# Fourier mixing and a gated SwiGLU on one Trainium2 core: gate rows on ScalarE, two splits four steps later, halves in the first item, raw weights one item sooner

## The chip, the core and the metric

The kernel runs on one core of a Trainium2 chip. Its engines run their own queues in order and meet at semaphores: TensorE (PE in the profile; PEld are its weight loads), VectorE (DVE), ScalarE (ACT), GpSimd (POOL) and SyncE (SP). In this kernel SP issues nearly all loads, POOL nearly all stores. The metric is the time of one execution on the device in microseconds (us); several runs are given by their median.

## The reference

`x` has 2048 rows of 512. The result mixes two branches by a gate of each row:

```python
g = sigmoid((x * gate_w).sum(-1, keepdims=True))
a = x @ dft_hid_re.T ; b = x @ dft_hid_im.T
y = dft_seq_re @ a - dft_seq_im @ b           # branch A, real part of a 2-D Fourier transform
out_B = (silu(x @ w1) * (x @ w3)) @ w2        # branch B, inner width 1376
result = g * y + (1 - g) * out_B
```

All is float32.

## The kernel before, in words

**Precision.** Each float32 operand is split in two: a high part (ScalarE copies it into the tensor engine's rounded format, `high`, line 107) and a low part (VectorE subtracts the high part from the source, `low`, line 110). `mm3` (line 124) then makes each product of three matmuls: high by high, high by low, low by high, in this order. `split` is `high` and then `low`; the profile shows all of them under lines 108 and 111 and all matmuls under line 122.

**Seven products in place of eight.** Each product of 2 x 2 blocks is done by a Strassen-like scheme with seven block products and some sums of blocks, made by VectorE ahead of the splits (`T1` to `T4`, `sums_wb`, `sums1`, `sum2`, `sum_c`).

**First half: gate/up.** The list `ITEMS` holds 22 items, a chunk of 128 columns of `w1` and `w3` by a half of the rows of x. Item 0 is written out by hand (lines 409 to 515, eight products). The others run in `gate_up(n)`, seven products of six matmuls. The order of instructions is the program's (`manual_schedule`): the dictionaries `early`, `ahead`, `second`, `mid` and `at_end` hang extra work into marked places of item n. Product numbers in `prod(ps, n, wi, xi, ...)`: weight forms 0 to 2 come from tile `wa`, 3 to 6 from tile `wb`; x forms are `OPS`, so 3 is `T1`, 4 `T2`, 5 `T3`, 6 `T4`. Products 0 and 1 of an item are done `LOOK` = 3 items ahead (`first1`, `first2`).

The forms of `wb` for the next set (`nw`) are made in the item before: `sums_wb` (four sums of 256 columns, VectorE, lines 253 to 256), `high_wb` (ScalarE, 1024 columns) and `low_wb` (VectorE, 1024 columns). Item 1 makes set 2 in this way, and the forms of `wa` for item 5. For sets below `K` = 9 the `wb` is stored to DRAM, and in the second half of the items (`back`) it is loaded again by `load_wb`; only the raw weights for `wa` (three quarters of a tile, 384 KB) come by `load_w`, four items ahead, at the start of `gate_up`, behind `load_wb` on SP's queue. The x operands of the first half are split during item 0 and 1: the low of `T1` in `early`, the split of `T4` in `ahead` of item 1.

**Second half: the transform.** It goes in blocks: four of the sequence transform (kind F), two of the down projection with `w2` (H) and two of the hidden transform (Y). A block has seven products in the order `CHAIN` (`P1`, `P5`, `P6`, `P3`, `P7`, `P2`, `P4`), each in a few steps; a step of block 0 is twelve matmuls. `step(m)` issues the matmuls of step m and then `advance(m)`: loads for step m + 8, the sum for step m + 4 (`sum_c`, lines 682 and 685) and the split of the operand `zo` for step m + 3 (`split_c`). Four buffers hold `zo`. `at(blk, n, f)` hangs extra work ahead of step n of a block.

The stationary operand of the F blocks is x itself, in eight blocks p of two x halves: `A1[p]` (four first forms, made during gate/up) and `A2[p]` (three second forms, made in block 0). For these, block 0 loads the x blocks again (`load_a2`, steps 4 to 11), makes one sum each (`sum2`, steps 7 to 14) and splits three forms (`make_a2` with `forms2`, steps 8 to 15): two forms of 256 columns in one split of 512, and one form of 256. Form 2 is first read by `P7` (steps 16 to 19), forms 0 and 1 by `P2` (from step 20) and `P4` (from 24). Buffers of the x blocks 4 and 5 are `u3` and `c21`.

**Gates.** The scores of the row gates are one more column of `w1`. `load_score` brings them to all partitions (SP for the first half of the rows, at the end of gate/up; POOL for the second, in block 1). `gates(g)` (line 760) makes them gates: a sigmoid (ScalarE, line 763), two rows of 512 each of a gate times -1 plus 1, or times 1 minus 1, written in the pairwise order of the output columns (VectorE, line 766), a sign change (ScalarE, line 769) and two stores (POOL). SP loads them again in `load_gate` ahead of `P6` of a block (line 854).

Of the kernel before, what the change touches and what calls it, by code (L numbers as in the profile page):

```python
# [9 lines left out]
AF = mybir.ActivationFunctionType  # L10
ALU = mybir.AluOpType
# [10 lines left out]
NG = NST // 2  # L22
NC = (F + P - 1) // P
NP2 = (NC + 1) // 2
WARM = 11
LOOK = 3
# [6 lines left out]
def fnet_swiglu_gate_kernel(  # L33
# [20 lines left out]
    nc = tc.nc  # L54
# [25 lines left out]
    def bank(k, name):  # L80
        return psum.tile([P, 512], F32, tag=f"ps{k}", name=name)
# [20 lines left out]
    def free(*tiles):  # L102
        for t in tiles:
            _, places, at = HELD.pop(id(t))
            places.append(at)

    def high(hi, src):
        nc.scalar.activation(hi, src, AF.Copy)  # L108

    def low(hi, lo, src):  # L110
        nc.vector.tensor_sub(lo, src, hi.bitcast(F32))  # L111

    def split(hi, lo, src):
        high(hi, src)
        low(hi, lo, src)
# [25 lines left out]
    def flat(ap):  # L141
        return ap.rearrange("p a n -> p (a n)")
# [30 lines left out]

        nc.vector.tensor_sub(r[:, :256], r[:, 256:512], r[:, :256])  # L174

    def forms2(r, t2):

        r = r.rearrange("p (a n) -> p a n", a=4)
        split(flat(t2[:, 0, 0:2]), flat(t2[:, 1, 0:2]), flat(r[:, 2:4]))
        split(t2[:, 0, 2], t2[:, 1, 2], r[:, 0])  # L180

# [6 lines left out]
    SETS, WSET = [], []  # L190
# [8 lines left out]
    def flat_x(ap):  # L199
        return ap.rearrange("p q n -> p (q n)")  # L200
# [15 lines left out]
    def xo_parts(g, k):  # L216
        o = XO[g][:, :, OPS.index(k)]
        return flat_x(o[:, 0]), flat_x(o[:, 1]), ST[g, k]

    def split_xo(g, k):  # L220
        split(*xo_parts(g, k))

    WS, WA, WB = {}, {}, {}

    def back(w):
        return w >= NC and SETS[w] > 0

    def load_w(w, lo=0, hi=4):
        if lo == 0:
            WS[w] = f4_a.tile([P, 4, 256], F32, tag=f"f4_{4 + w % (LOOK + 1)}", name=f"ws{w}")  # L230
        nc.sync.dma_start(WS[w][:, lo:hi].rearrange("p a n -> p (a n)"),
                          w13[SETS[w], :, lo * 256 : hi * 256])

    def load_wb(w, spare=False):

        WB[w] = (parts(f"wb{w}") if spare else
                 wbp.tile([P, 2, 4, 256], F32R, tag="wb", name=f"wb{w}"))
        nc.sync.dma_start(WB[w].bitcast(F32), wbsp[SETS[w]])
# [4 lines left out]
    def new_wa(w):  # L243

        WA[w] = wap.tile([P, 2, 3, 256], F32R, tag="wa", name=f"wa{w}")

    WU = {}

    def sums_wb(w):

        r = WS.pop(w)
        u = WU[w] = wup.tile([P, 4, 256], F32, tag="wu", name=f"wu{w}")
        nc.vector.tensor_add(u[:, 0], r[:, 3], r[:, 2])
        nc.vector.tensor_sub(u[:, 1], u[:, 0], r[:, 0])
        nc.vector.tensor_sub(u[:, 2], r[:, 0], r[:, 3])
        nc.vector.tensor_sub(u[:, 3], r[:, 1], u[:, 1])

    def wb_parts(w):
        return flat(WB[w][:, 0]), flat(WB[w][:, 1]), flat(WU[w])

    def high_wb(w):
        WB[w] = wbp.tile([P, 2, 4, 256], F32R, tag="wb", name=f"wb{w}")
        high(wb_parts(w)[0], wb_parts(w)[2])

    def low_wb(w):
        low(*wb_parts(w))
        if w < K:
            nc.gpsimd.dma_start(wbsp[w], WB[w].bitcast(F32))

    def prod(ps, n, wi, xi, start, chain=False):  # L270
        w = WSET[n]
        w, wi = (WA[w], wi) if wi < 3 else (WB[w], wi - 3)
        x = XO[ITEMS[n][1]]
        for q in range(2):
            sl = slice(q * P, (q + 1) * P)
            mm3(ps, w[:, 0, wi, sl], w[:, 1, wi, sl], x[:, 0, xi, q, :], x[:, 1, xi, q, :],
                start and q == 0, q == 1, chain)
# [3 lines left out]
    def first1(n):  # L281
        copy_x(n, prod1(n))
# [46 lines left out]
    def store_h(n, k, h):  # L329

        c, g = ITEMS[n]
        j = min(c % (NP2 - 1) if c < NC - 1 else NP2 - 1, NP2 - 1)
        b = 2 * (NP2 - 1 <= c < NC - 1)
        nc.gpsimd.dma_start(hsp[g, b + k, j // 2, :, j % 2 * 512 : (j % 2 + 1) * 512], h)  # L334
# [4 lines left out]
    early, ahead, second, mid, at_end = {}, {}, {}, {}, {}  # L339

    def run(work, n):
        for f in work.get(n, ()):
            f()

    def gate_up(n):
        last = NI - 1
        x, s1 = G.pop(n)
        z = bank(6 + n % 2, f"Z{n}")
        if n == last - 1:

            u2, g1 = (s1p.tile([P, 512], F32, tag="s1", name=f"{k}_{n}") for k in ("u2", "g1"))
        else:
            h = hp.tile([P, 1024], F32, tag="h", name=f"h{n}")
            u2, g1 = h[:, :512], h[:, 512:]
        u4 = u4p.tile([P, 512], F32, tag="u4", name=f"u4_{n}")
        nw = WSET[n + 1] if n < last else 0
        if nw in WB or nw == 0:
            nw = None
        elif back(nw):
            load_wb(nw)  # L360
            nw = None
        wa = WSET[n + LOOK + 1] if n + LOOK < last else 0
        if wa in WA or wa == 0:
            wa = None
        else:
            load_w(wa, 0, 3 if back(wa) else 4)

        prod(x, n, 4, 4, False, True)
        nc.scalar.activation(u2, x, AF.Copy)
        run(early, n)  # L370
        prod(z, n, 5, 5, True, True)
        run(ahead, n)
        nc.scalar.activation(u4, z, AF.Copy)
        run(second, n)
        if nw is not None:
            sums_wb(nw)
        if n + LOOK <= last:
            first1(n + LOOK)
        if nw is not None:
            high_wb(nw)  # L380
        prod(x, n, 3, 3, False, True)
        nc.vector.tensor_add(u4, u4, x)
        if nw is not None:
            low_wb(nw)
        run(mid, n)
        prod(z, n, 2, 6, False, True)
        nc.vector.tensor_add(u2, u2, z)
        nc.vector.tensor_mul(u2, s1, u2)  # L388
        store_h(n, 0, u2)
        if wa is not None:  # L390
            new_wa(wa)
            parts_a = wa_parts(wa, 0, 3)
            high(parts_a[0], parts_a[2])
        if n + LOOK <= last:
            first2(n + LOOK)
        if wa is not None:
            low(*parts_a)
        prod(x, n, 6, 2, False, True)
        nc.scalar.activation(g1, x, AF.Silu)
        put_score(n, 1, x)  # L400
        if n + LOOK <= last:
            gate1(n + LOOK)
        nc.vector.tensor_mul(g1, g1, u4)
        store_h(n, 1, g1)
        run(at_end, n)
# [36 lines left out]
    def xo_half(k, q):  # L442
        i = OPS.index(k)
        return XO[0][:, 0, i, q], XO[0][:, 1, i, q], ST[0, k][:, q * 512 : (q + 1) * 512]
# [72 lines left out]
    def do(work, n, f, *a):  # L517
        work.setdefault(n, []).append(lambda: f(*a))


    do(early, 1, lambda: low(*xo_parts(0, "T1")))
    do(ahead, 1, lambda: split_xo(0, "T4"))
    do(second, 1, free, *(ST[0, b] for b in ("B11", "B21", "B12", "B22")))
    do(second, 1, sum_g, 2, y2)
    do(mid, 1, gate1, 2)
# [48 lines left out]
    A1, A2, XR = [], [], {}  # L574
# [17 lines left out]
    for n in range(NI):  # L592
        if n in W2_AT:
            p = W2_AT.index(n)
# [4 lines left out]
        if n in A1_AT:  # L599
            p = A1_AT.index(n)  # L600
# [9 lines left out]
    n = NI - 1 - LOOK  # L610
# [117 lines left out]
    def load_a2(p):  # L728
# [8 lines left out]
            XR[p] = wide(f"xs{p}")  # L737
        nc.sync.dma_start(XR[p], xn[p])

    def make_a2(p):  # L740
        A2.append(a2.tile([P, 2, 3, 256], F32R, tag=f"a2_{p}", name=f"a2_{p}"))
        r = XR.pop(p)
        forms2(r, A2[p])
        if p >= NG - 2:
            free(r)

    GATES = {}

# [10 lines left out]

    def gates(g):  # L760

        t, ng = GATES.pop(g)
        nc.scalar.activation(t, t, AF.Sigmoid)
        for j, (v, w) in enumerate(((-1.0, 1.0), (1.0, -1.0))):
            b = slice(j * 512, (j + 1) * 512)
            nc.vector.tensor_scalar(ng[:, b].rearrange("p (n a) -> p a n", a=2),
                                    t[:, b].rearrange("p (a n) -> p a n", a=2),
                                    v, w, op0=ALU.mult, op1=ALU.add)
        nc.scalar.activation(t[:, 512:], t[:, 512:], AF.Copy, scale=-1.0)
        nc.gpsimd.dma_start(gsp[g], t)  # L770
        nc.gpsimd.dma_start(ngsp[g], ng)
# [197 lines left out]
    def at(blk, n, f, *a):  # L969
        todo.setdefault(START[blk] + n, []).append((f, a))  # L970
# [5 lines left out]
        at(0, 7 + p, lambda p=p: sum2(XR[p]))  # L976
    for p in range(NG):
        at(0, 8 + p, make_a2, p)

    at(0, 0, lambda: nc.scalar.activation(act0, act0, AF.Sigmoid))  # L980
    at(0, 4, gates, 0)
    at(1, 3, gates, 1)
    late = [(w2, w2sp, p) for p in range(len(W2_AT), NP2)] + [(dd, dsp, p) for p in range(KD)]
    for i, (src, sp, p) in enumerate(late):
        blk, b = 1 + i // 3, i % 3
        n = (10, 17, 24)[b]
# [11 lines left out]
    for p in range(KD):  # L998
        early = p < NG - NP2
# [76 lines left out]
```

## Time and profile before

| | |
|---|---|
| median of three runs | 678.73 us (678.22 to 678.82) |
| the profiled execution's own time | 678.22 us |
| its span, first to last instruction | 676.5 us |
| TensorE busy | 671.2 us (99%), 3101 matmuls |
| TensorE weight loads busy | 582.8 us (86%) |
| VectorE busy | 602.5 us (89%) |
| ScalarE busy | 365.8 us (54%) |
| GpSimd busy | 64.5 us (10%) |
| DMA | 172.54 MB, 255 GB/s in the mean |
| granted TensorE clock | 1.000 |

How to read the lines below. A row of a timeline has the start in us, the time taken, engine and source line, the operation, the tile written and the tiles read, shapes and a count x; in brackets stands the idle time of the engine ahead of it and what ended it. Rows with x over 1 are merged neighbours. A busy matmul shows about 0.38 us because matmuls are pipelined; what counts is how far apart they start. A view of waits gives engine, line, tile, what was waited for, and then us in total, times and longest. The chain goes back from the last instruction by what released each one.

### The profile page before, as it was taken

Reading aid. Unit: us, or ns where it says so; the run is one execution under the profiler, and the core shown is the slowest. Engines: PE = TensorE matmul, PEld = TensorE weight load, DVE = VectorE, ACT = ScalarE, POOL = GpSimd, SP = SyncE. Lnnn points to the kernel's source line nnn. Section 1 sums busy time; section 2 is a strip of 40 time slices with the busy share of each in tenths; the row PEclk is TensorE's granted clock in tenths of the full one; section 3 lists DMA queues with packets and bytes.
Section 4 is the critical chain, followed back from the end, with each engine's and each line's share of the span. In section 5 each row is a group of like instructions: output and inputs, shape, how many; then the busy total and the mean of one; then the engine's idle time right before and its main releaser. Section 6 shows DMA issues by size and latency. Waiting matters only on the chain.

```text
span 676.5 us, 8652 instructions
## 1 busy us (share of the span) xinstructions
PE 671.2 (99%) x3101; PEld 582.8 (86%) x3101; DVE 602.5 (89%) x739; ACT 365.8 (54%) x479; POOL 64.5 (10%) x119
## 2 busy tenths in 40 slices
PE   9999999999999999999999999999999999999998
PEld 6888888888888888888888888888888888888887
DVE  6999988787679999988999899979796897898996
ACT  6675666655446764465554653554445445445551
POOL 0011111121110000001120101100000010000000
PEclk9999999999999999999999999999999999999999
DMA  7575557499998656814697178919986772874942
GB/s 295 207 305 219 218 194 276 184 328 381 420 415 314 240 181 229 315 69 179 241 352 285 74 253 336 374 56 353 391 328 249 291 244 100 311 271 159 338 134 93
DMA packets 45563, 172.54 MB, mean 255 GB/s; under 512 B 5328, under 2 KB 5712, under 8 KB 41680
## 3 DMA queue, kind: packets, MB, share of 16 engines
q1 hardware_dynamic: 32480, 118.11, 47.9%
q0 software_dynamic: 12752, 53.49, 20.1%
q8 instruction: 24, 0.39, 0.2%
q10 hardware_dynamic: 288, 0.39, 0.2%
q14 instruction: 19, 0.16, 0.1%
HBM read 114.82 MB, written 57.16 MB: 254 GB/s over the span
## 4 chain that ended last, share of the span: by engine, by line
PE 87%; DVE 8%; DMA 1%; issue 1%; ACT 1%; SPq 0%; DVEq 0%; ACTq 0%
PE P L122 61%; PE X L122 15%; PE Z L122 8%; PE Y L122 3%; DVE zo L111 3%; DVE a L111 1%; DMA xs_B<-xt 1%; DVE B L682 1%; DVE B L685 1%; DVE wa L111 1%; DVE xs_B L214 1%; DVE xs L174 0%; DVE xo L111 0%; ACT zo L108 0%; DMA out<-zc 0%
## 5 line engine op out<-in xcount | busy, mean ns | idle before, releaser
L122 PE MATMUL P<-zo,a 128*128 128x512 f32 x1344 | 290.9, 379 | 1.0 <-DVE zo L111 1.0
L122 PEld LDWEIGHTS P<-zo,a 128*128 128x128 f32 x1344 | 253.5, 189 | 38.3 <-DVE zo L111 2.4
L108 ACT ACTIVATE zo<-B 128x1024 fp32r<-128x1024 f32 (+1 forms) x182 | 188.2, 1041 | 180.6 <-PE P L122 79.3
L111 DVE TENSOR_TENSOR zo<-B,zo 128x1024 fp32r<-128x1024 f32 (+1 forms) x182 | 217.0, 1200 | 29.4 <-ACT zo L108 28.8
L122 PE MATMUL P<-zo,H 128*128 128x512 f32 x468 | 101.2, 379 | 0.0
L122 PEld LDWEIGHTS P<-zo,H 128*128 128x128 f32 x468 | 88.5, 189 | 12.6
L682 DVE TENSOR_TENSOR B<-B,B 128x1024 f32<-128x1024 f32 (+1 forms) x78 | 92.7, 1188 | 0.1
L122 PE MATMUL X<-xo,wb 128*128 128x512 f32 x378 | 89.0, 380 | 0.2 <-DVE xo L111 0.2
L122 PEld LDWEIGHTS X<-xo,wb 128*128 128x128 f32 x378 | 71.2, 189 | 11.1 <-DVE xo L111 0.6
L122 PE MATMUL P<-zo,Y 128*128 128x512 f32 (+1 forms) x336 | 71.6, 375 | 0.0
L122 PEld LDWEIGHTS P<-zo,Y 128*128 128x128 f32 x336 | 62.7, 189 | 8.7
L334 POOL DMA_DIRECT2D hsp<-h x42 | 23.0, 548 | 120.4 <-DVE h L388 68.0
L685 DVE TENSOR_TENSOR B<-B,B 128x1024 f32<-128x1024 f32 x26 | 31.6, 1217 | 0.0
L122 PE MATMUL X<-xo,wa 128*128 128x512 f32 x126 | 30.9, 380 | 0.0
L122 PE MATMUL Y<-xo,wa 128*128 128x512 f32 x126 | 30.6, 379 | 0.0
L122 PE MATMUL Z<-xo,wa 128*128 128x512 f32 x126 | 30.6, 379 | 0.0
L122 PE MATMUL Z<-xo,wb 128*128 128x512 f32 x126 | 30.6, 379 | 0.0
L122 PEld LDWEIGHTS X<-xo,wa 128*128 128x128 f32 x126 | 23.7, 189 | 3.8 <-DVE wa L111 0.5
L122 PEld LDWEIGHTS Y<-xo,wa 128*128 128x128 f32 x126 | 23.8, 189 | 3.4
L122 PEld LDWEIGHTS Z<-xo,wb 128*128 128x128 f32 x126 | 23.8, 189 | 3.4
L122 PEld LDWEIGHTS Z<-xo,wa 128*128 128x128 f32 x126 | 23.8, 189 | 3.4
L111 DVE TENSOR_TENSOR wa<-ws,wa 128x768 fp32r<-128x768 f32 (+1 forms) x22 | 19.3, 880 | 8.1 <-ACT wa L108 8.0
(145 smaller groups left out, 543.8 us busy)
## 6 DMA issues: line engine op xcount, KB each, us to landing
B<-cc SPq DMA_DIRECT2D x64, 512.0 KB, 6.0
hsp<-h POOLq DMA_DIRECT2D x42, 256.0 KB, 3.6
B<-hsp SPq DMA_DIRECT2D x20, 512.0 KB, 5.6
wbsp<-wb POOLq DMA_DIRECT2D x8, 1024.0 KB, 4.2
wb<-wbsp SPq DMA_DIRECT2D x8, 1024.0 KB, 7.7
B<-zsp SPq DMA_DIRECT2D x16, 512.0 KB, 8.4
H<-w2sp SPq DMA_DIRECT2D x6, 1024.0 KB, 9.5
ws<-w SPq DMA_DIRECT2D x11, 512.0 KB, 4.6
```

What stands on the lines that cost most here:

```text
L108: nc.scalar.activation(hi, src, AF.Copy)
L111: nc.vector.tensor_sub(lo, src, hi.bitcast(F32))
L122: nc.tensor.matmul(ps.rearrange("p (n a) -> p n a", a=2), u, turns(v)[:, some], **kw)
L214: nc.vector.tensor_sub(t, *(ST[g, v] for v in SUMS[k]))
L334: nc.gpsimd.dma_start(hsp[g, b + k, j // 2, :, j % 2 * 512 : (j % 2 + 1) * 512], h)
L682: nc.vector.tensor_add(t, t, RAW[blk, b, q][:, :n])
L685: nc.vector.tensor_sub(t, RAW[blk, "B12", q], t)
```

## The change

- `forms2` takes a set `some`, and can make the split of 512 columns (0) and that of 256 (1) apart. For x blocks 4 and 5 (`IN_TWO`) `make_a2` makes only the second, at its old place (steps 12 and 13), and `rest_a2` the first, ahead of steps 16 and 17.
- `gates` is taken apart. The sigmoid goes from step 4 of block 0 to step 2; the two rows are made by ScalarE (`gate_row`), one ahead of step 3 and one ahead of step 4; the sign change and the stores (`store_gates`) come ahead of step 5. In block 1, where all was ahead of step 3: sigmoid 3, rows 4 and 5, rest 6.
- `wb_parts` gives two halves of 512 columns, so `high_wb` and `low_wb` issue two instructions each, for every set they make.
- In item 1 the u sum (line 382) comes ahead of `sums_wb` and `high_wb`, and the low parts of `T1` and `T4` are made in halves.
- For the last four sets (16 to 19) `load_w` is issued in the item before the one that issued it, behind the other loads at the start of `gate_up`.

```diff
-    def forms2(r, t2):
+    def forms2(r, t2, some):
         r = r.rearrange("p (a n) -> p a n", a=4)
-        split(flat(t2[:, 0, 0:2]), flat(t2[:, 1, 0:2]), flat(r[:, 2:4]))
-        split(t2[:, 0, 2], t2[:, 1, 2], r[:, 0])
+        if 0 in some:
+            split(flat(t2[:, 0, 0:2]), flat(t2[:, 1, 0:2]), flat(r[:, 2:4]))
+        if 1 in some:
+            split(t2[:, 0, 2], t2[:, 1, 2], r[:, 0])
...
     def wb_parts(w):
-        return flat(WB[w][:, 0]), flat(WB[w][:, 1]), flat(WU[w])
+        return [(flat(WB[w][:, 0, i:j]), flat(WB[w][:, 1, i:j]), flat(WU[w][:, i:j]))
+                for i, j in ((0, 2), (2, 4))]
     def high_wb(w):
...
-        high(wb_parts(w)[0], wb_parts(w)[2])
+        for v in wb_parts(w):
+            high(*v[::2])
     def low_wb(w):
-        low(*wb_parts(w))
+        for v in wb_parts(w):
+            low(*v)
...
-        else:
+        elif wa not in WS:
             load_w(wa, 0, 3 if back(wa) else 4)
+        w = WSET[min(n + LOOK + 2, last)]
+        if w - LOOK - 1 >= NC + 1 and w not in WS and w not in WA:
+            load_w(w, 0, 3)
...
-        if nw is not None:
+        if nw is not None and n > 1:
             sums_wb(nw)
         if n + LOOK <= last:
             first1(n + LOOK)
-        if nw is not None:
+        if nw is not None and n > 1:
             high_wb(nw)
         prod(x, n, 3, 3, False, True)
         nc.vector.tensor_add(u4, u4, x)
+        if nw is not None and n == 1:
+            sums_wb(nw)
+            high_wb(nw)
         if nw is not None:
             low_wb(nw)
...
+    def low_halves(k):
+        for q in range(2):
+            low(*xo_half(k, q))
-    do(early, 1, lambda: low(*xo_parts(0, "T1")))
-    do(ahead, 1, lambda: split_xo(0, "T4"))
+    do(early, 1, low_halves, "T1")
+    do(ahead, 1, lambda: high(*xo_parts(0, "T4")[::2]))
+    do(ahead, 1, low_halves, "T4")
...
+    IN_TWO = (NG - 4, NG - 3)
     def make_a2(p):
...
-        r = XR.pop(p)
-        forms2(r, A2[p])
+        forms2(XR[p], A2[p], (1,) if p in IN_TWO else (0, 1))
         if p >= NG - 2:
-            free(r)
+            free(XR.pop(p))
+    def rest_a2(p):
+        forms2(XR.pop(p), A2[p], (0,))
...
     def gates(g):
+        nc.scalar.activation(GATES[g][0], GATES[g][0], AF.Sigmoid)
+    def gate_row(g, j):
+        t, ng = GATES[g]
+        v = 2.0 * j - 1.0
+        b = slice(j * 512, (j + 1) * 512)
+        nc.scalar.activation(ng[:, b].rearrange("p (n a) -> p a n", a=2),
+                             t[:, b].rearrange("p (a n) -> p a n", a=2),
+                             AF.Copy, scale=v, bias=-v)
+    def store_gates(g):
         t, ng = GATES.pop(g)
-        nc.scalar.activation(t, t, AF.Sigmoid)
-        for j, (v, w) in enumerate(((-1.0, 1.0), (1.0, -1.0))):
-            b = slice(j * 512, (j + 1) * 512)
-            nc.vector.tensor_scalar(ng[:, b].rearrange("p (n a) -> p a n", a=2),
-                                    t[:, b].rearrange("p (a n) -> p a n", a=2),
-                                    v, w, op0=ALU.mult, op1=ALU.add)
         nc.scalar.activation(t[:, 512:], t[:, 512:], AF.Copy, scale=-1.0)
...
+    for n, p in enumerate(IN_TWO):
+        at(0, 16 + n, rest_a2, p)
...
-    at(0, 4, gates, 0)
-    at(1, 3, gates, 1)
+    for g in range(2):
+        at(g, 2 + g, gates, g)
+        for j in range(2):
+            at(g, 3 + g + j, gate_row, g, j)
+        at(g, 5 + g, store_gates, g)
```

## The prediction

> **What bounds the kernel now.** I read the page first, then who made TensorE wait, then the chain of waits in order of time, and last the timelines of the two places that this pointed to.
>
> ```profile
> span 676.5 us, 8652 instructions
> ```
> ```profile
> PE P L122 <- DVE zo L111: 1.0, 2, 0.7
> PE wps L414 <- PEq L1065: 0.8, 1, 0.8
> PE X L122 <- DVE xo L111: 0.2, 1, 0.2
> ```
> ```profile
> 254.80 1.15 DVE zo L111
> 255.95 0.04 issue
> 255.99 414.57 PE P L122 x1919
> ```
>
> The profiled execution took 678.22 us: its span of 676.5 and 1.7 around it. The first view has every wait of TensorE that VectorE ended, three in all. The second, the chain, shows that from 255.99 us on nothing but matmuls sets the end: 414.57 / 1919 = 0.216 us for each, one 512-column matmul after another. So whatever the change does behind 256 us is worth nothing unless it makes a new wait, and what it can gain lies ahead of that. Two places lose time there.
>
> The first is the second item of gate/up (TensorE's timeline):
>
> ```profile
> 28.04 0.38 PE L122 MATMUL X<-xo,wb 128*128 128x512 f32 x1
> 28.59 1.35 PE L122 MATMUL X<-xo,wb 128*128 128x512 f32 x5 [0.18 <-DVE xo L111]
> 29.78 1.46 PE L122 MATMUL Z<-xo,wa 128*128 128x512 f32 x6
> 31.07 1.46 PE L122 MATMUL Y<-xo,wa 128*128 128x512 f32 x6
> 32.47 2.88 PE L122 MATMUL X<-xo,wb 128*128 128x512 f32 x12
> 35.19 1.46 PE L122 MATMUL Z<-xo,wb 128*128 128x512 f32 x6
> 36.48 1.66 PE L122 MATMUL X<-xo,wa 128*128 128x512 f32 x6
> ```
>
> Starts should be 0.216 apart, and a group of six busy 5 x 0.216 + 0.38 = 1.46. The one at 28.04 is followed after 0.55: 0.34 lost. The five behind it take 1.35 for 1.24: 0.11. From 31.07 six matmuls should end the turn at 32.37, not 32.47: 0.10. The twelve take 2.88 for 2.76: 0.12. The six at 36.48 take 1.66 for 1.46: 0.20. Together 0.87 us. That is the head's share.
>
> The second is the first transform block:
>
> ```profile
> 207.62 44.47 PE L122 MATMUL P<-zo,a 128*128 128x512 f32 x205
> 252.78 2.86 PE L122 MATMUL P<-zo,a 128*128 128x512 f32 x12 [0.69 <-DVE zo L111]
> 255.99 6.31 PE L122 MATMUL P<-zo,a 128*128 128x512 f32 x28 [0.35 <-DVE zo L111]
> ```
>
> 205 x 0.216 = 44.28, so the next should start at 251.90; it starts at 252.78: 0.88 lost. Twelve more are due at 255.37 and come at 255.99: 0.62. The 28 take 6.31 for 6.21: 0.10. Together 1.60 us. No more than 0.87 + 1.60 = 2.47 us can be gained at these places.
>
> **Transform: gate rows and moved forms.** One step is 12 matmuls, 2.59 us, so 207.62 is step 0, and steps 17 and 18 are the late ones: each waits for VectorE's low part of its operand, and VectorE runs without a break up to there.
>
> ```profile
> 221.55 0.84 DVE L766 TENSOR_SCALAR u2g<-p5g 128x512 f32<-128x512 f32 x2
> 222.26 1.21 DVE L682 TENSOR_TENSOR B<-B,B 128x1024 f32<-128x1024 f32 x1
> 224.09 1.23 DVE L111 TENSOR_TENSOR zo<-B,zo 128x1024 fp32r<-128x1024 f32 x1 [0.62 <-ACT zo L108]
> ...
> 254.72 3.64 DVE L111 TENSOR_TENSOR zo<-B,zo 128x1024 fp32r<-128x1024 f32 x3
> ```
> ```profile
> 216.07 1.07 ACT L108 ACTIVATE zo<-B 128x1024 fp32r<-128x1024 f32 x1 [1.20 <-DVE B L682]
> 218.34 1.07 ACT L108 ACTIVATE zo<-B 128x1024 fp32r<-128x1024 f32 x1 [1.20 <-DVE B L682]
> 219.31 1.06 ACT L929 ACTIVATE zs<-P 128x512 f32<-128x512 f32 x2
> 220.27 1.05 ACT L763 ACTIVATE p5g<-p5g 128x1024 f32<-128x1024 f32 x1
> 222.49 0.63 ACT L769 ACTIVATE p5g<-p5g 128x512 f32<-128x512 f32 x1 [1.17 <-DVE u2g L766]
> ```
>
> Removed from VectorE: the two rows of line 766. The sum at 222.26 starts 0.71 after them and would start where they do. ScalarE no longer stands 1.17 waiting for them ahead of line 769, so step 7's high part comes earlier and VectorE's idle 0.62 (row 224.09) goes as well: 0.71 + 0.62 = 1.33.
>
> Added to ScalarE, one a step: sigmoid 1.05 at step 2, where it stood idle 1.20 ahead of 216.07; one gate row at step 3, in the idle 1.20 ahead of 218.34; the other at step 4, in the place the sigmoid leaves. No row shows this row of alternating columns on ScalarE; the nearest with as many elements is 0.63 (L769), and the other bound is a row of twice as many, 1.05. I take 0.63. The second row then ends by 220.90 and step 7's high part by 221.97; the sum for step 8, which VectorE does meanwhile, ends at 221.55 + 1.21 = 222.76, so even at 1.05 nothing waits. Without the cover each row would put 0.63 ahead of a high part. The stores of the gates go one step later in the program but earlier in time, since what they wait for is earlier, and SP's gate load and the x loads queued behind it with them.
>
> Moved from steps 12 and 13 to 16 and 17: one 512-column split of each of two x blocks. Its price on VectorE is that of a half:
>
> ```profile
> 5.46 1.29 DVE L111 TENSOR_TENSOR xo<-xs_B,xo 128x512 fp32r<-128x512 f32 x2 [0.15 <-ACT xo L108]
> ```
>
> Two halves take 1.29 where one ends 0.69 after its start, so one starts 0.60 after the other. Twice 0.60 leaves the path to step 18: 1.33 + 1.20 = 2.53 us earlier than the row 254.72, whose end decides step 18. TensorE wants to be 1.50 earlier there (0.88 + 0.62), so step 18 has 1.0 us in hand. Step 17 was 0.88 late and has 1.6. ScalarE's highs don't become the pace: each goes ahead as VectorE's sums do, and its PSUM reads wait for TensorE at times that lie before the lows need them.
>
> What is late next: the two moved splits come back at 16 and 17, ahead of the lows of steps 19 and 20. The first of the three lows at 254.72 now starts at 252.19; with a pitch of 1.13 and 0.60 for the moved one, step 19's starts at 253.92 and ends at 255.14, and TensorE, unstalled, comes for it at 207.62 + 19 x 2.592 = 256.87. So they hide, and all 1.60 us go.
>
> This holds if TensorE waits for the part of a tile that it reads. Step 18 reads the third form of the very x blocks whose first two are now written at 16 and 17:
>
> ```profile
> L122 PE MATMUL C<-xo,wa x6: 379/379/484, 8.4 to 9.7; 128*128 128x512 f32 x6
> L111 DVE TENSOR_TENSOR wa<-ws,wa x1: 422/422/422, 9.4 to 9.4; 128x256 fp32r<-128x256 f32 x1
> ```
>
> In the first item matmuls read one part of `wa` from 8.4 on, though a write to another part, ahead of them in the program, starts at 9.4. The wait goes by parts.
>
> **Head: halves and the order of the sums.** VectorE's timeline:
>
> ```profile
> 27.32 1.22 DVE L111 TENSOR_TENSOR xo<-t,xo 128x1024 fp32r<-128x1024 f32 x1
> 28.53 1.23 DVE L111 TENSOR_TENSOR xo<-xs_B,xo 128x1024 fp32r<-128x1024 f32 x1
> 29.67 0.68 DVE L305 TENSOR_TENSOR s<-s,Y 128x512 f32<-128x512 f32 x1
> 30.27 0.42 DVE L253 TENSOR_TENSOR wu<-ws 128x256 f32<-128x256 f32 x1
> ...
> 31.73 0.68 DVE L382 TENSOR_TENSOR u<-u,X 128x512 f32<-128x512 f32 x1
> 32.94 1.23 DVE L111 TENSOR_TENSOR wb<-wu,wb 128x1024 fp32r<-128x1024 f32 x1 [0.53 <-ACT wb L108]
> 34.08 0.68 DVE L387 TENSOR_TENSOR h<-h,Z 128x512 f32<-128x512 f32 x1
> ...
> 36.01 0.95 DVE L111 TENSOR_TENSOR wa<-ws,wa 128x768 fp32r<-128x768 f32 x1
> ```
> ```profile
> 31.85 1.06 ACT L108 ACTIVATE wb<-wu 128x1024 fp32r<-128x1024 f32 x1 [2.38 <-DVE wu L256]
> ```
>
> The low of T1 starts at 27.32 and held TensorE until it ended. Its first half ends at 28.01, before the matmul due at 28.26: 0.34 + 0.11 go. The u sum now stands ahead of the four weight sums, which took 30.27 to 31.73, so the 0.10 at 32.37 (TensorE waits to write the bank that this sum reads) goes. But TensorE then reaches the six at 36.48 earlier, and their third matmul needs the low of `wa` at 36.01, which is VectorE's chain. That chain, new: T1's halves 27.32 to 28.52, T4's 28.53 to 29.73, the sum of L305 to 30.33, the u sum to 30.93, the four weight sums (1.46) to 32.39. ScalarE's high of the first half needs two of them, by 31.85, and ends about 0.6 later, at 32.45; the second runs 32.5 to 33.1. Lows 32.48 to 33.08 and 33.13 to 33.73. Line 387 started at 34.08: 0.35 earlier, and so is `wa`. Of 0.87 the head gains 0.35; the rest turns into a longer wait at the six. Bounds: 0, if halves cost more than here; 0.87, if `wa` is early enough.
>
> [...]
>
> **Edits at nothing.** In the other items the weight halves cost some 0.07 each on VectorE, against the 0.53 it stood waiting for the whole high, which halves shorten; TensorE has no wait between 37 and 205 us. The raw weights of the last four sets go one item sooner on SP, behind the load of `wb` and into a free buffer. They hide behind that load's slack:
>
> ```profile
> wb<-wbsp SPq DMA_DIRECT2D x8, 1024.0 KB, 7.7
> ```
>
> It lands after 7.7 us, an item is 42 matmuls, 9.07. Only the first of the four adds traffic (384 KB, each later one replaces another); at the page's mean of 255 GB/s that is up to 1.5 us once, which is no more than the slack plus a tenth. Gain or loss: 0 to 0.1.
>
> **Sum.** 1.60 + 0.35 = 1.95 us. From the profiled execution's 678.22 that gives 676.27; that run is the lowest of three whose median is 678.73, and a median of the new kernel should lie as far above its lowest: 678.73 - 1.95 = 676.8.
>
> **Rivals.**
> - The head gains nothing (two halves at 0.69 each instead of 1.29 together, or the new wait at `wa` takes all): 678.73 - 1.60 = 677.1.
> - The head gains all: 678.73 - 2.47 = 676.3. Against it: the chain to 36.01 above.
> - TensorE waits for the whole x tile. Step 18 then waits for the split at step 17: 253.92 + 1.13 + 0.69 = 255.74 where it is due at 254.28, 1.5 lost again, net 0.45: 678.3. The rows of `wa` speak against it.
> - The time freed does not become lead, because ScalarE paces the highs: one of the two stalls (0.72 with its restart) stays, and the head gains nothing beside it: 678.73 - 0.88 = 677.8.
> - The sigmoid, two steps sooner, waits for its scores. All of ScalarE's highs queue behind it.
>
> ```profile
> xs<-xn SPq DMA_DIRECT2D x8, 512.0 KB, 11.8
> p5g<-gs SPq DMA_DIRECT2D x1, 512.0 KB, 5.4
> ```
>
> The scores, issued at 207.8, land 5.4 later, at 213.2, and the sigmoid now wants to start at 214.9. With the 11.8 of the x loads issued right behind them they would land at 219.6; sigmoid 1.05, high part 1.07, low 1.22 make step 5 ready at 222.9 where TensorE is at 220.8: 2.2 lost, and the lead of later steps with it, some 0.5 more: 678.73 + 2.7 - 1.95 = 679.5. It stalls from a landing of 217.5 on and loses to the kernel before from about 219. Against it: nothing ahead of that load changes, and the traffic that delays the x loads is queued behind it.
>
> **How the numbers follow.** Forecast 0.56, head nothing 0.13, head all 0.10, whole tile 0.08, ScalarE paces 0.07, sigmoid waits 0.06. The first three gain over 0.2% (1.36 us, about what a measurement of this kernel can tell from no change): 0.79, less 0.06 for a median that falls short by chance: faster 0.73. The next two with that 0.06: same 0.21. The last: slower 0.06. The range runs from the full gain on the lowest run shown (678.22 - 2.47 = 675.8, taken as 675.9) to 678.6, which takes in the whole-tile case and leaves out the sigmoid's.
>
> **What would show it.** Right: no wait of TensorE on `zo` between 249 and 256 us, step 18 about 1.6 earlier against step 0; no gap behind 28.04; a wait of about 0.5 near 36 on the low of `wa`. Wrong: a TensorE wait that names the low of `a` at step 18; ScalarE waiting for the scores' DMA ahead of the sigmoid; a wait for `wb` between 140 and 180 us; new waits past 256.

## The result and the profile after

The changed kernel takes 676.05 us in the median of six runs (675.79 to 676.97), against 678.75 for six of the kernel before (678.22 to 679.20). The ratio is 0.9964, 95% interval 0.9954 to 0.9974: 2.70 us less. The profiled execution took 676.03 with a span of 674.3, against 678.22 and 676.5, so the two profiles are 2.19 apart; where most of the other 0.5 probably comes from is told with the raw weights below. On a later chip the pair stood at 676.16 and 678.40.

TensorE's waits after the change, the whole answer of that view but its heads (engine, line, what was waited for, us in total, times, longest):

```profile
PE wps L425 <- PEq L1095: 0.8, 1, 0.8
```

Only the start of the warm-up is left; the three waits on VectorE are gone. (A matmul shows 0.38 us busy, so one that starts less than 0.16 late leaves no idle time and isn't in this view; such losses are read from the starts, as below.) The page's chain by engine, before and after:

```profile
PE 87%; DVE 8%; DMA 1%; issue 1%; ACT 1%; SPq 0%; DVEq 0%; ACTq 0%
```
```profile
PE 99%; DMA 0%; DVE 0%; ACT 0%; issue 0%
```

VectorE had 8% of what set the end and has none now. That is the length of the path that ran over VectorE, some 54 us of 676.5, and not the time lost to it. The transform, TensorE's timeline of the changed kernel:

```profile
207.04 55.21 PE L122 MATMUL P<-zo,a 128*128 128x512 f32 x255
```

254 starts of 0.216 and one matmul of 0.38 make 55.24: no loss in the first 255, where 1.60 us were lost. VectorE around the steps that had been late:

```profile
251.52 1.22 DVE L111 TENSOR_TENSOR zo<-B,zo 128x1024 fp32r<-128x1024 f32 x1
252.66 0.69 DVE L111 TENSOR_TENSOR a<-xs,a 128x512 fp32r<-128x512 f32 x1
253.26 1.22 DVE L111 TENSOR_TENSOR zo<-B,zo 128x1024 fp32r<-128x1024 f32 x1
254.40 0.69 DVE L111 TENSOR_TENSOR a<-xs,a 128x512 fp32r<-128x512 f32 x1
255.00 1.22 DVE L111 TENSOR_TENSOR zo<-B,zo 128x1024 fp32r<-128x1024 f32 x1
```

The first row is step 18's low part. It ends at 252.74; TensorE is there with its second matmul at 207.04 + 18 x 2.592 + 0.216 = 253.91, so it is 1.2 us early. Counted from step 0 the row starts 2.62 us sooner than in the kernel before (47.10 us behind it then, 44.48 now). The two `a` rows are the moved splits, 0.60 apart from what follows them, and step 18 reads other parts of the same tiles without waiting for them: TensorE loses nothing there.

ScalarE where the gate rows went:

```profile
214.19 1.04 ACT L782 ACTIVATE p5g<-p5g 128x1024 f32<-128x1024 f32 x1
215.49 1.07 ACT L108 ACTIVATE zo<-B 128x1024 fp32r<-128x1024 f32 x1 [0.27 <-DVE B L698]
216.46 0.85 ACT L788 ACTIVATE u2g<-p5g 128x512 f32<-128x512 f32 x1
217.74 1.06 ACT L108 ACTIVATE zo<-B 128x1024 fp32r<-128x1024 f32 x1 [0.43 <-DVE B L698]
218.70 1.06 ACT L954 ACTIVATE zs<-P 128x512 f32<-128x512 f32 x2
219.66 0.90 ACT L788 ACTIVATE u2g<-p5g 128x512 f32<-128x512 f32 x1
220.35 1.07 ACT L108 ACTIVATE zo<-B 128x1024 fp32r<-128x1024 f32 x1
```

The sigmoid and the first row end while ScalarE would still wait for VectorE's sum (0.27 and 0.43 of idle are left). A row takes 0.85 to 0.90, not 0.63.

The head, TensorE and then VectorE:

```profile
28.15 1.46 PE L122 MATMUL X<-xo,wb 128*128 128x512 f32 x6
29.45 1.46 PE L122 MATMUL Z<-xo,wa 128*128 128x512 f32 x6
30.74 1.46 PE L122 MATMUL Y<-xo,wa 128*128 128x512 f32 x6
32.04 2.75 PE L122 MATMUL X<-xo,wb 128*128 128x512 f32 x12
34.63 1.46 PE L122 MATMUL Z<-xo,wb 128*128 128x512 f32 x6
35.92 1.63 PE L122 MATMUL X<-xo,wa 128*128 128x512 f32 x6
```
```profile
27.02 1.29 DVE L111 TENSOR_TENSOR xo<-t,xo 128x512 fp32r<-128x512 f32 x2
28.23 1.29 DVE L111 TENSOR_TENSOR xo<-xs_B,xo 128x512 fp32r<-128x512 f32 x2
29.44 0.68 DVE L310 TENSOR_TENSOR s<-s,Y 128x512 f32<-128x512 f32 x1
30.04 0.68 DVE L390 TENSOR_TENSOR u<-u,X 128x512 f32<-128x512 f32 x1
30.64 0.42 DVE L255 TENSOR_TENSOR wu<-ws 128x256 f32<-128x256 f32 x1
...
32.21 1.37 DVE L111 TENSOR_TENSOR wb<-wu,wb 128x512 fp32r<-128x512 f32 x2
33.50 0.68 DVE L398 TENSOR_TENSOR h<-h,Z 128x512 f32<-128x512 f32 x1
...
35.42 0.95 DVE L111 TENSOR_TENSOR wa<-ws,wa 128x768 fp32r<-128x768 f32 x1
```

Every group but the last takes its 1.46 or 2.75. The last takes 1.63: 0.17 lost at the low of `wa`. From T1's low to that of `wa` VectorE takes 35.42 - 27.02 = 8.40 us where it took 36.01 - 27.32 = 8.69: 0.29 shorter. This execution also began that stretch 0.30 sooner, already at 22.59 against 22.89, behind loads that had landed 0.3 sooner. That is a difference between executions: in the five other profiles with this head T1's low began at 27.16 to 27.44, where it began at 27.02 here.

### The profile page after: what moved, and what is told of

Its sections match the earlier page's. It is cut to its first block, busy times and chain, and to the rows that moved or that the text cites. A ratio compares the mean times of both kernels' runs of the same rounds, so it can differ in the third digit from the quotient of the medians.

```text
span 674.3 us, 8670 instructions
## 1 busy us (share of the span) xinstructions
PE 670.3 (99%) x3101; PEld 583.8 (87%) x3101; DVE 601.5 (89%) x748; ACT 370.4 (55%) x494; POOL 64.5 (10%) x119
## 4 chain that ended last, share of the span: by engine, by line
PE 99%; DMA 0%; DVE 0%; ACT 0%; issue 0%
PE P L122 68%; PE X L122 16%; PE Z L122 8%; PE Y L122 4%; PE C L122 2%; PE wps L425 1%; DMA out<-zc 0%; DVE zc L856 0%; ACT zc L863 0%
## 5 line engine op out<-in xcount | busy, mean ns | idle before, releaser
L954 ACT ACTIVATE zu<-P 128x512 f32<-128x512 f32 x30 | 17.7, 596 | 15.2 <-PE P L122 12.7
```

The costliest lines, as they stand in the source:

```text
L954: nc.scalar.activation(U[name][:, r], ps[r], AF.Copy)
```

## The experiments

All times are medians, each beside the kernel before on the same chip; ratios have their 95% interval, which is about 0.6 us to either side. "Restart" is the 0.10 us that nearly every wait of TensorE in these traces costs beside itself: the second matmul behind it starts 0.32 us after the first and not 0.216. Two profiles also differ for reasons that are no edit's. The first product's matmul starts at 5.41 to 6.54 us, as its load lands, and that start and the losses up to 26 us, put together, range over 0.5 us in thirteen of the fourteen profiles (the last, of the order alone, is 0.5 later still).

**One part alone: the transform.** `forms2`, `make_a2`, `rest_a2` and the gates as changed, the rest as before.

> Gate rows by ScalarE and the moved splits, with the first item and the raw weights as before. Theory: the transform's 1.60 us go whole and the head's 0.87 stay, so 1.6 us faster than before and no wait of TensorE on zo between 249 and 256 us. Rival (ScalarE paces the high parts): one late step stays, 0.9 us faster. Rival (the gain needs the head's earlier start): under 1 us.

Measured 677.14 against 678.62, ratio 0.9978 (0.9969 to 0.9986): 1.48 us. No wait of TensorE on `zo`. The transform's share is what the sum made it. But a wait stood where before's profile had none (TensorE):

```profile
180.45 1.46 PE L122 MATMUL Z<-xo,wb 128*128 128x512 f32 x6
182.32 1.64 PE L122 MATMUL X<-xo,wa 128*128 128x512 f32 x6 [0.41 <-ACT h L401]
```

The second should start at 180.45 + 1.30 = 181.75. It is 0.57 late and loses 0.18 more inside. The bank (a piece of TensorE's result memory) that this second group writes was last read by the silu of line 401, and on ScalarE the silu stands behind the high of `wa`:

```profile
180.94 0.84 ACT L108 ACTIVATE wa<-ws 128x768 fp32r<-128x768 f32 x1 [4.25 <-DMA ws<-w]
181.68 0.58 ACT L401 ACTIVATE h<-X 128x512 f32<-128x512 f32 x1
```

ScalarE waits 4.25 us for the last raw weights, and the silu with it; of the 0.18 inside the group 0.10 is the restart, and the low of `wa`, made behind the high and done only at 182.77, may have cost the rest. In the first profile of before the same wait ended a little sooner:

```profile
179.61 0.84 ACT L108 ACTIVATE wa<-ws 128x768 fp32r<-128x768 f32 x1 [3.86 <-DMA ws<-w]
```

There TensorE lost nothing.

**One part alone: the head.** Halves and the order of the sums.

> Halves and the u sum first, with the transform and the raw weights as before. Theory: VectorE's chain up to the low of wa gets 0.3 us shorter, and the time 0.3 to 0.4 us; the wait at wa near 36 us takes the rest of the 0.87. Rival (the head gains all it lost): 0.8 us or more. Rival (halves cost what they save): 0.

Measured 678.34 against 678.62, ratio 0.9997 (0.9988 to 1.0006). By time alone that is no difference that can be told; the median has the size that the theory gives, and the profile has its form: VectorE's stretch to the low of `wa` is 35.78 - 27.39 = 8.39, 0.30 shorter, and TensorE's only loss between 28 and 40 us is at that low (0.48 and 0.10 of restart, 0.58 for 0.87).

The starts of the matmuls in all profiles say more than this one time. Between 26 and 45 us TensorE loses 0.56 to 0.88 us in the five profiles with the head as before (0.76 in the mean), and 0.17 to 0.58 in the six with both edits (0.38). The difference, 0.37, has the forecast's size; the 0.87 that the prediction started from was at the upper end of what executions lose there.

**Either half of the transform's part.** Gate rows by ScalarE without the moved splits, and the moved splits without the rows.

> Gate rows by ScalarE, splits not moved, first item as before. Theory: VectorE is 1.33 us earlier, step 18 wants 1.50, so one short wait of about 0.2 plus 0.1 of restart stays at step 18 and none at 17: 1.3 us faster. Rival (the moved splits do the work, the rows are hidden anyway): under 0.5 us.

> The moved splits alone, gate rows on VectorE as before. Theory: 1.20 us earlier at step 18, which wants 1.50, so a wait of about 0.3 plus 0.1 stays there and none at 17: 1.2 us faster. With rows_only's share that is more than the whole, since either alone nearly does it. Rival (the parts add up): the two together give 1.6, so 0.3 here if the rows give 1.3.

Measured 677.47 (0.9984, 0.9975 to 0.9993) and 677.39 (0.9982, 0.9974 to 0.9991) against 678.62: 1.15 and 1.23 us. TensorE's timeline of the moved splits alone:

```profile
208.04 47.01 PE L122 MATMUL P<-zo,a 128*128 128x512 f32 x217
255.21 3.07 PE L122 MATMUL P<-zo,a 128*128 128x512 f32 x13 [0.16 <-DVE zo L111]
```

The next start was due at 208.04 + 217 x 0.216 = 254.91: 0.30 at step 18 and none at 17, as worked out. With the rows alone the wait at step 18 is 0.11, and 0.10 of restart. The parts don't add up: each does most of it (1.15 and 1.23 of 1.48), and the second takes the rest.

**The raw weights.**

```diff
-        else:
+        elif wa not in WS:
             load_w(wa, 0, 3 if back(wa) else 4)
+        w = WSET[min(n + LOOK + 2, last)]
+        if w - LOOK - 1 >= NC + 1 and w not in WS and w not in WA:
+            load_w(w, 0, 3)
```

Alone (`raw_only`), and the changed kernel without it (`no_raw`):

> The raw weights one item sooner and nothing else. In all four kernels that leave this part out TensorE now stood 0.5 to 0.75 us near 182 us, at the low part of the last set's wa, whose raw weights landed 10.0 to 10.2 us after their issue; in the one profile of before they took 8.9 and it did not stand. Theory (this wait is the usual case): 0.5 to 0.7 us faster than before, and no wait near 182. The prediction's own term: 0, never more than 0.1 slower.

> The changed kernel with the raw weights loaded as before. Theory: 0.5 to 0.7 us slower than the changed kernel (676.05), so 676.6 to 676.8, 0.27 to 0.30 percent under before, with the wait near 182 us. The prediction's own term: 676.05 again.

Measured 678.19 against 678.61, ratio 0.9993 (0.9984 to 1.0001), and 676.88, ratio 0.9974 (0.9965 to 0.9983), where the whole change had 0.9964 and 0.9967. That is 0.4 us in the one. In the other it is 0.5 or 1.0, by which of the two measurements of the whole change one takes, each against the kernel before beside it. The first interval still holds 1, and the second overlaps both of the whole change's, so by time alone the gain isn't clear of noise and its size is rough; the profiles below are the better evidence. The trace of the first has no wait near 182 us and no wait for the weights on ScalarE:

```profile
176.78 0.84 ACT L108 ACTIVATE wa<-ws 128x768 fp32r<-128x768 f32 x1 [0.64 <-PE Z L122]
```

It lost 0.28 at 187 us instead, which no other kernel showed: VectorE, and with it the sum that frees a bank, stood 3.29 us for blocks of x that landed late. The profile of `no_raw` happened to have no wait near 182 (its last raw weights landed 9.1 us after their issue), so its median, not its profile, speaks; it lies just above the 676.6 to 676.8 that was expected. Of the eight profiles of kernels with the late load, six have the wait, 0.5 to 0.75 us each: all with a landing of 9.9 us or more. The two without it landed after 8.9 and 9.1. Of the six with the sooner load none has it. But the next transfer in line is near in all six. ScalarE's copy into `h`, one item on, waits until an earlier store of `h` to DRAM has landed, which takes 9.0 to 10.6 us from its issue here and took 7.2 to 8.2 with the late load. ScalarE stands 0.7 to 2.3 us for it, and once, in the run `wa_sooner` below, that reached TensorE.

**Halves alone, and the order alone.** The first leaves the four weight sums ahead of the u sum, the second (below) leaves `wb`, T1 and T4 whole.

```diff
-        if nw is not None:
+        if nw is not None and n > 1:
             sums_wb(nw)
...
         nc.vector.tensor_add(u4, u4, x)
+        if nw is not None and n == 1:
+            sums_wb(nw)
+            high_wb(nw)
```

> Halves of wb, T1 and T4, but the four weight sums stay ahead of the u sum. Theory: VectorE's idle 0.53 ahead of the low of wb goes because the high of the first half is done while the u sum runs, so the chain to wa gets as short as with both, and the time gains 0.3 us like head_only; TensorE waits about 0.1 at the u sum's bank before it meets wa. Rival (the order of the sums is what counts): 0.

> The u sum ahead of the weight sums, without halves. Theory: ScalarE's whole high (1.06) then starts only when all sums are done and nothing covers it on VectorE, so the low of wb starts about 0.5 later than before, and with it the low of wa: 0.3 to 0.6 us slower than before, with the wait near 37 us grown by as much. Rival (it gains its 0.1): 0.1 faster.

Halves alone: 678.56 against 678.61, ratio 1.0000 (0.9991 to 1.0008). A miss: the chain to `wa` got even shorter (35.12 - 26.90 = 8.22), but TensorE now stood longer at the bank that the u sum reads:

```profile
32.13 2.86 PE L122 MATMUL X<-xo,wb 128*128 128x512 f32 x12 [0.22 <-DVE u L385]
```

Y before it started at 30.46, so 31.76 was due: 0.38 lost and 0.10 behind it. I had put 0.1 there. The order alone: 679.54, ratio 1.0015 (1.0006 to 1.0023), 0.9 us slower. VectorE and TensorE show why:

```profile
34.17 1.23 DVE L111 TENSOR_TENSOR wb<-wu,wb 128x1024 fp32r<-128x1024 f32 x1 [1.12 <-ACT wb L108]
```
```profile
35.45 1.13 PE L122 MATMUL X<-xo,wb 128*128 128x512 f32 x4 [0.56 <-DVE wb L111]
```

VectorE stands 1.12 us for the whole high where it stood 0.53, and the low of `wb` itself becomes what TensorE waits for; the stretch to the low of `wa` is 37.23 - 27.94 = 9.29, 0.60 longer, the upper end of what was expected, and the time lost more than that. The profile doesn't put all of the 0.9 in the head: TensorE lost 1.22 us between 26 and 45 us for the 0.87 of before, and at 354 us 0.29 more than before, at a low part whose own delay stays open.

So the order alone loses: it frees the bank and uncovers ScalarE's high, and the halves cover that again. Whether the halves alone gain is open. Their median shows 0.05 us, within 0.6 either way; their profile loses 0.48 in the head, less than each of the five with the head as before (0.56 to 0.88) and within what the six with both edits lose (0.17 to 0.58).

**The rest of the head's loss.** In item 1 alone, the low of `wa` comes directly behind the sum of line 398; the product of line 399 and the gate sum, which stood between them on VectorE, now come behind the low:

```diff
         nc.vector.tensor_add(u2, u2, z)
-        nc.vector.tensor_mul(u2, s1, u2)
-        store_h(n, 0, u2)
         if wa is not None:
             new_wa(wa)
             parts_a = wa_parts(wa, 0, 3)
             high(parts_a[0], parts_a[2])
+        if wa is not None and n == 1:
+            low(*parts_a)
+        nc.vector.tensor_mul(u2, s1, u2)
+        store_h(n, 0, u2)
         if n + LOOK <= last:
             first2(n + LOOK)
-        if wa is not None:
+        if wa is not None and n > 1:
             low(*parts_a)
```

> The changed kernel with the low of wa, in item 1 alone, ahead of the product of line 399 and of the gate sum instead of behind both. Theory (the wait moved from the u sum's bank to wa): it is ready 0.6 to 1.2 us sooner, TensorE has no wait near 36 us, 0.2 to 0.35 us faster than the changed kernel. Rival (what is put behind it is late next): no gain, a wait elsewhere before 45 us.

> The changed kernel once more, beside the three below on one chip: 675.8 to 676.4 us, no wait near 182 us, one of 0.2 to 0.4 near 36 us at the low of wa.

Measured 676.61, and 676.16 for the changed kernel beside it: 0.4 us slower in the medians, within the intervals (0.9961 to 0.9984, and 0.9955 to 0.9980). The traces bear out the rival; the times are too close to tell. The group at the low of `wa` takes its 1.46, and the next is late:

```profile
36.05 1.46 PE L122 MATMUL X<-xo,wa 128*128 128x512 f32 x6
37.78 1.56 PE L122 MATMUL X<-xo,wb 128*128 128x512 f32 x6 [0.28 <-ACT h L377]
```

Due at 37.35, it comes 0.43 late, for a copy on ScalarE that stands behind the gate's silu, which waits for the sum put behind `wa`. Another 0.34 went near 183 us in this execution, for the store of `h` named with the raw weights, issued at 171.90 and landed at 182.52:

```profile
182.62 0.60 ACT L377 ACTIVATE h<-X 128x512 f32<-128x512 f32 x1 [2.27 <-DMA hsp<-h]
183.27 1.56 PE L122 MATMUL X<-xo,wb 128*128 128x512 f32 x6
```

So not all of the difference in time is the edit's. The changed kernel itself came as expected, with 0.28 lost near 36 us. No version beat it.

**Which engine makes the gate rows.** On VectorE at the new places; and on ScalarE twice each.

> The changed kernel with the two gate rows by VectorE at the new places (steps 3 and 4). Theory: 0.7 us of the 1.14 in hand at step 18 go, 0.4 stay, no wait of TensorE, the time of the changed kernel. With the splits moved the engine of the rows doesn't matter. Rival (the rows' engine is what counts): 0.7 us slower.

> The changed kernel with each gate row made twice by ScalarE. Theory: the rows lie in ScalarE's idle time, the second copies too or nearly; the time of the changed kernel. Rival (ScalarE paces the high parts): up to 1.2 us slower per block, with step 7's high part late.

Measured 676.27 and 676.43 for 676.16 of the changed kernel beside them, all three with ratio 0.9967 (0.9955 to 0.9980). With the rows on VectorE step 18's low part is

```profile
252.35 1.22 DVE L111 TENSOR_TENSOR zo<-B,zo 128x1024 fp32r<-128x1024 f32 x1
```

and ends at 253.57, 0.46 ahead of TensorE (this execution's block starts at 207.16, so 207.16 + 46.66 + 0.22 = 254.03). The theory had 0.4. Twice the rows on ScalarE make step 7's high part 1.3 us late and use 0.6 of the 1.2 us to spare at step 18, and TensorE still doesn't wait.

## Why the prediction was right, and where its sizes were off

**Bounds.** That only the stretch ahead of 256 us counts held: behind it the matmuls run as before.

**Transform, 1.60.** Held: 1.61 between the two profiles (207.62 - 207.04 = 0.58 at the block's start, 2.19 at the end) and 1.48 in the time of the part alone. Its steps held too: step 18's low part was to come 2.53 us earlier and came 2.62, for 1.50 wanted; there were to be 1.0 us to spare, and there were 1.2; the moved splits come back under cover; step 18 waited for no other part of its tiles (255 matmuls in an unbroken 55.21 us), so the whole-tile rival falls. One price was low: the gate row on ScalarE was put at 0.63 and took 0.85 to 0.90; it lay within the bound of 1.05 and was covered, and doubling it changed nothing. The rivals of ScalarE's pace and of the waiting sigmoid fall with the same rows. What I hadn't said is that each of the two edits does most of it alone, 1.15 and 1.23.

**Head, 0.35.** The mechanism held: no gap behind 28.15, and the loss ends up at the low of `wa`. The chain shortened by 0.29 to 0.30, since the second pair of halves and the wait between the `wb` halves cost a little more than I gave them. The part alone has 0.28, an interval that doesn't exclude 0; the 0.37 between the losses of the profiles with and without both edits is the better evidence. The wait left at `wa`, forecast as about 0.5, was 0.17 to 0.58 in six profiles with both of these edits, depending on how early TensorE and VectorE began. Pairs of these halves of which the second waits for nothing take 1.28 or 1.29 in the profiles, not twice 0.69, so the first rival's case of 0.69 for each half falls. In item 1 the pair of `wb` takes 1.36 or 1.37 where both edits are in, but its second half waits for ScalarE's second high, which in the profile after ends at 32.86, just ahead of it.

**Raw weights, 0.** This is the term that was mis-sized, and probably most of why 676.8 was forecast for 676.05. The step was "Gain or loss: 0 to 0.1". I had looked for a price and costed the edit by what its traffic could delay; that TensorE had no wait between 37 and 205 us I read from one execution, in which the landing was early by some tenths. It is worth 0.4 to 1.0 us by times that are rough, and 0.5 to 0.75 in each execution that has the wait. That the median of before lay 0.5 over its profiled execution fits this, since six of eight profiles have the wait; the unprofiled executions show no waits, so it isn't shown for them. The prediction's bound of 2.47 us left this place out, and the whole change gained 2.70 and 2.24. The profile of before showed ScalarE waiting 3.86 us for that load, with a TensorE bank behind it, and I took a wait that reached nobody for one that costs nothing.

The three parts alone give 1.48 + 0.28 + 0.42 = 2.18, each with some 0.6 either way; the pair measured last on one chip is 678.40 - 676.16 = 2.24 apart, the first pair 2.70.

## What to carry to other kernels

Where a profile is one execution and its time is the lowest of several, look at the waits that just miss the bounding engine: a long wait for a load on an engine whose next instruction frees a bank can be a stall in the executions that the profile doesn't show: in the profile of before ScalarE's 3.86 us cost nothing, and in six of the eight profiles with that late load such a wait cost TensorE 0.5 to 0.75 us. Removing it can bring up the next transfer behind it, as the store of `h` did here (0.34 us, once). Where two edits each shorten the same chain, compare each one's gain with what the late step wants, not their sum; the second may only buy slack. Halving an operand and changing the order of sums belong together when the one uncovers what the other hides: the order alone lost 0.9 us here.

## What the runs showed of the hardware

- A 512-element copy on ScalarE that writes every other float took 0.85 to 0.91 us (L788 in the profile after, L788 and L791 in the one with the rows made twice), while one that writes them side by side took 0.63 (L769 before). On VectorE two such rows held up the next instruction by 0.71 us in the kernel before, so 0.36 each.
- The same 384 KB load, issued at the same place, landed 8.9 to 10.3 us later in eight executions.
- The second matmul behind a wait of TensorE started 0.32 us after the first, for 0.216 in an unbroken row (behind 252.78 and 255.99 in the kernel before, behind 36.43 in the changed one).
